# Attention exponentials: values two pairs behind their scores, and a polynomial over 2 x 112 columns in place

## Chip, core and metric

The kernel runs on one core of one Trainium2 chip. The metric is the device time of one launch in microseconds; it is measured in several executions, and one more execution is profiled. The core has five engines with queues of their own: PE (matrix products, into PSUM), ACT (functions such as the exponential), DVE (elementwise work), POOL (elementwise work on SBUF alone, and the issue of some DMAs) and SP (issue of the other DMAs).

## What is computed

The reference mixes attention over 2048 tokens (16 heads of 28 columns) with a mixture of eight experts, by a gate of one number per token:

```python
def _A_ref(x, wqkv, wo):
    B, S, D = x.shape
    H = 16; Dh = D // H
    qkv = (lambda x, *d: x.transpose(*d))((x @ wqkv).reshape(B, S, 3, H, Dh), 2, 0, 3, 1, 4)
    q, k, v = qkv[0], qkv[1], qkv[2]
    scale = Dh ** -0.5
    scores = jnp.einsum("bhqd,bhkd->bhqk", q, k) * scale
    p = _softmax(scores, axis=-1)
    o = jnp.einsum("bhqk,bhkd->bhqd", p, v)
    return (lambda x, *d: x.transpose(*d))(o, 0, 2, 1, 3).reshape(B, S, D) @ wo
...
x = A_x
g = _sigmoid((x * gate_w).sum(-1, keepdims=True))
a = _A_ref(x, A_wqkv, A_wo)
b = _B_ref(x, B_w_gate, B_w1, B_w2)
return g * a + (1 - g) * b
```

The change touches the attention alone: the exponentials of the scores and their product with the values.

## The kernel before

The program first makes q, k and v, then runs the experts (with row maxima of the scores beside them), and then the attention as a stage of its own. The work of the attention is cut into 16 units u: four groups of four heads, and in each four blocks of 512 queries. A unit has eight pairs p of key tiles, a tile being 128 keys; `m` counts the pairs from 0 to 127. The softmax is not normalised in the loop: the row maximum is part of the scores' matmul (a 29th row of K and Q), so the exponential is safe, and a column of ones in V sums it.

For one pair, `scores(m)` writes eight cells of 128 keys x 512 queries (two key tiles, four heads). They go into all eight PSUM banks: for the first key tile the single bank `z[0]` and the three banks of `t[0]`, for the second the three of `t[1]` and the single `z[1]`. Each cell takes three matmul passes (high and low parts of K and Q). ACT then does exp on `z[0]` (L1230), on the three banks of `t[0]` at once (L1231), and on those of `t[1]` (L1239). The cell `z[1]` is copied by DVE into SBUF as `X`, scaled (L1232); of X, ACT does the first 352 columns (L1240), and the last PW = 160 go through a polynomial, `power`: four steps on POOL (L1246 to L1251) that split the exponent off, and four on DVE (L1253, L1254, L1255 and L1257) that evaluate it and write `P[:, 7]`. `P` holds the eight exponentials of a pair and has two buffers.

`values(m)` multiplies P by V into the same single banks `z[0]` (columns 0 to 287 of the queries) and `z[1]` (288 to 511) at L1271, and DVE adds both to the accumulator `osb` of the unit (L1281, or a copy at L1279 for a unit's first pair). So one round on PE is scores of pair m+1, then values of pair m; a single bank goes from scores to ACT's or DVE's read, to values, to DVE's add, and to the next scores.

The order on PE, DVE, ACT and POOL is the order in which the code is written (`manual_schedule`); SP's order is made by the scheduler. Beside the pairs, `beside(m)` places the work of other units: sums of a unit's exponentials go to memory and back to be inverted (`collect_sums`, `slice_sums`, `invert_sums`, `spread_sums`, the last fetching the row `rs`), `divide_half` divides osb by them two units later, `place` stores osb into `OT`, K, V and Q of the next group are loaded (`load_k`, `load_v`, `load_q`), and wo and OT are split into high and low parts. POOL's DMAs wait in the list `due`, from which each `power` takes one behind its third POOL step. At the end stand the 16 projections with wo (L1137).

Of the kernel before, what the change touches and what calls it, by code (L numbers as in the profile page):

```python
# [63 lines left out]
def tile_gated_mha_moe(ctx: ExitStack, tc: tile.TileContext, x, xe_, xT, wv, wqk, wo, w1, w2, out):  # L64
# [1037 lines left out]
    def split_wo_high(b):  # L1102
        nc.vector.tensor_copy(wo_h[:, b], wo_r[b])
# [60 lines left out]
    def divide_half(u, h):  # L1164
        cs = slice(256 * h, 256 * h + 256)
        nc.vector.tensor_tensor(accs[u][:, cs], accs[u][:, cs], rs[u][:, cs], op=ALU.mult)
# [26 lines left out]
    PW = 160  # L1193
# [24 lines left out]
    def scores(m):  # L1218
# [3 lines left out]
        X = sb.tile([128, 512], F32, name="X")  # L1222
        P = sb.tile([128, 8, 512], F32, name="P")
# [6 lines left out]
        nc.scalar.activation(P[:, 0], z[0], AF.Exp, scale=SCALE)  # L1230
        nc.scalar.activation(P[:, 1:4], t[0], AF.Exp, scale=SCALE)  # L1231
        nc.vector.tensor_scalar(X, z[1], LAM * SCALE * math.log2(math.e), -126.0 * LAM, op0=ALU.mult, op1=ALU.max)  # L1232
# [6 lines left out]
        nc.scalar.activation(P[:, 4:7], t[1], AF.Exp, scale=SCALE)  # L1239
        nc.scalar.activation(P[:, 7, 0:512 - w], X[:, 0:512 - w], AF.Exp, scale=math.log(2.0) / LAM)  # L1240
        Pc[m] = [P[:, i] for i in range(8)]

    def power(x, to):
        u, n, g, y = (sb.tile([128, PW], F32, name=f"p{c}", bufs=1 + (c == "u")) for c in "ungy")
# [8 lines left out]
        nc.vector.scalar_tensor_tensor(y, g, EXP2[0], g, op0=ALU.add, op1=ALU.mult)  # L1253
        nc.vector.scalar_tensor_tensor(v, y, EXP2[1], g, op0=ALU.add, op1=ALU.add)  # L1254
        nc.vector.scalar_tensor_tensor(w, y, EXP2[2], v, op0=ALU.add, op1=ALU.mult)  # L1255
        yield
        nc.vector.scalar_tensor_tensor(to, w, EXP2[3], e.bitcast(F32), op0=ALU.add, op1=ALU.mult)  # L1257

    def values(m):
# [13 lines left out]
        if p == 0:  # L1273
            accs[u] = sb.tile([128, 512], F32, name="osb", bufs=4)
        for n, (po, cs) in enumerate(parts):
            if n:
                piece(u, p)
# [4 lines left out]

    def piece(u, p):
        if u > 1 and p in (2, 3):
            divide_half(u - 2, p - 2)

    def beside(m):
# [17 lines left out]
        if p == 0 and 5 <= u < 9:  # L1305
            split_wo_high(u - 5)
# [102 lines left out]
```

## Time and profile before

| | |
|---|---|
| time, median of 3 runs (lowest, highest) | 1333.95 us (1333.61, 1334.13) |
| the profiled execution: its own time | 1334.03 us |
| its span, first to last instruction | 1332.2 us |
| granted clock of TensorE | 1.00 |
| attention stage, first to last L1230 | 833.23 to 1287.97 us |
| mean of L1231 and L1239 (1536 columns) | 1446 and 1460 ns |
| mean of L1230 (512) and L1240 (352) | 600 and 509 ns |
| mean of the four DVE steps of the polynomial | 320, 325, 339, 317 ns |
| mean of the four POOL steps | 353, 329, 545, 375 ns |

The profile gives each instruction's start and duration, and what the idle time of its engine ahead of it waited for ("idle before, releaser"). In a row of groups stand line, engine, operation, output and inputs, shape, count, then busy us, mean ns, and the idle us by releaser. In a row of the timeline stand start and duration in us, then the same names. A duration isn't always what an instruction costs its engine: the next one can start before the former has ended, so distances from start to start are looked at too.

### The profile page before, as it was taken

The numbers are of one execution on the slowest core, as the hardware profiler recorded it, in microseconds if no ns is written. First come the engines' busy times: TensorE is split into PE (matmuls) and PEld (weight loads), VectorE is DVE, ScalarE is ACT, GpSimd is POOL, SyncE is SP. The second block draws the span as 40 slices with busy tenths as digits, with TensorE's granted clock in tenths as the row PEclk, the third lists the DMA queues.
The fourth block names the chain that finished last, engine by engine and source line by source line (L and its number), as shares of the span: only waits on it lengthen the run. The fifth ranks groups of instructions, "written<-read, shape, count | busy, mean of one in ns | idle before, by whom it ended". The sixth has DMA issues, their size and how long they took to land. (4 is left out here: it accounts for less than half of the span.)

```text
span 1332.2 us, 32345 instructions
## 1 busy us (share of the span) xinstructions
PE 1325.2 (99%) x12210; PEld 936.9 (70%) x12210; DVE 1064.0 (80%) x1667; ACT 843.5 (63%) x1271; POOL 856.7 (64%) x1142
## 2 busy tenths in 40 slices
PE   9999999999999999999999999999999999999999
PEld 8888788788887777777777777555555555555558
DVE  5746899888898888989888786777788778777775
ACT  5325454355364344543445434999999999999981
POOL 2143967877787788786887844666666666656641
PEclk9999999999999999999999999999999999999999
DMA  9887657554553475455746423212422432242214
GB/s 349 301 268 267 185 162 187 153 151 109 166 157 86 149 203 149 137 125 155 187 120 184 93 78 68 62 39 64 121 54 70 113 81 49 76 111 54 49 41 137
DMA packets 139520, 176.83 MB, mean 133 GB/s; under 512 B 25576, under 2 KB 107242, under 8 KB 138850
## 3 DMA queue, kind: packets, MB, share of 16 engines
q1 hardware_dynamic: 120626, 145.68, 36.0%
q0 software_dynamic: 18592, 28.84, 10.5%
q8 instruction: 96, 1.57, 0.5%
q14 instruction: 62, 0.51, 0.1%
q10 hardware_dynamic: 144, 0.23, 0.1%
HBM read 124.54 MB, written 53.25 MB: 133 GB/s over the span
## 5 line engine op out<-in xcount | busy, mean ns | idle before, releaser
L149 DVE TENSOR_REDUCE mp<-pm 128x3 f32<-128x1536 f32 (+1 forms) x301 | 508.9, 1733 | 10.9 <-PE pm L128 10.8
L1271 PE MATMUL z<-P,V 128*32 128x288 f32 x4064 | 247.9, 382 | 1.0 <-ACT P L1230 0.2
L1271 PEld LDWEIGHTS z<-P,V 128*32 128x32 f32 x4064 | 110.2, 109 | 132.7 <-ACT P L1230 48.5
L1065 ACT ACTIVATE yo<-acc,cg 128x448 f32<-128x448 f32 x64 | 40.7, 636 | 232.1 <-PE acc L1050 222.7
L833 POOL TENSOR_TENSOR w2l<-w2r,w2h 128x448 fp32r<-128x448 f32 x112 | 130.6, 1167 | 86.1 <-ACT w2h L827 64.9
L762 PE MATMUL s<-Q,Kh 29*128 29x512 f32 x1524 | 185.7, 437 | 0.0
L1239 ACT ACTIVATE P<-s 128x1536 f32<-128x1536 f32 x127 | 185.4, 1460 | 0.0
L1231 ACT ACTIVATE P<-s 128x1536 f32<-128x1536 f32 x127 | 183.6, 1446 | 0.0
L762 PE MATMUL z<-Q,Kh 29*128 29x512 f32 x508 | 182.7, 438 | 0.0
L1050 PE MATMUL acc<-w2h,hh 128*128 128x448 f32 x448 | 167.0, 373 | 0.3 <-PEq L847 0.3
L1050 PE MATMUL acc<-w2h,hl 128*128 128x448 f32 x448 | 166.5, 372 | 0.0
L1050 PE MATMUL acc<-w2l,hh 128*128 128x448 f32 x448 | 166.1, 371 | 0.0
L997 ACT ACTIVATE hf<-acc 128x512 f32<-128x512 f32 (+6 forms) x154 | 74.3, 482 | 136.5 <-PE acc L993 130.6
L142 DVE TENSOR_REDUCE mp<-acc 128x1 f32<-128x512 f32 x130 | 89.5, 688 | 83.9 <-PE pm L128 81.8
L842 POOL TENSOR_TENSOR hl<-hf,hh 128x512 fp32r<-128x512 f32 x112 | 145.9, 1303 | 1.1 <-ACT hh L1000 0.5
L993 PE MATMUL acc<-xeh,w1h 128*128 128x512 f32 (+3 forms) x408 | 136.8, 339 | 0.0
L993 PE MATMUL acc<-xeh,w1l 128*128 128x512 f32 (+3 forms) x408 | 136.1, 338 | 0.0
L1246 POOL TENSOR_SCALAR pu<-X 128x160 f32<-128x160 f32 x126 | 44.4, 353 | 132.7 <-DVE X L1232 131.2
L1281 DVE TENSOR_TENSOR osb<-z,osb 128x288 f32<-128x288 f32 x224 | 95.1, 425 | 41.6 <-PE z L1271 31.9
L1232 DVE TENSOR_SCALAR X<-z 128x512 f32<-128x512 f32 x127 | 87.8, 691 | 44.5 <-PE z L762 30.8
L801 POOL TENSOR_TENSOR w1l<-w1r,w1h 128x1024 fp32r<-128x1024 f32 (+1 forms) x49 | 91.1, 1860 | 43.7 <-ACT w1h L795 24.2
L128 PE MATMUL pm<-khg,qg 28*128 28x512 f32 x894 | 110.5, 449 | 0.9 <-DVE lo L672 0.9
(238 smaller groups left out, 3072.4 us busy)
## 6 DMA issues: line engine op xcount, KB each, us to landing
w2r<-in_w_dram SPq DMA_DIRECT2D x112, 224.0 KB
w1r<-in_w_dram SPq DMA_DIRECT2D x56, 384.0 KB
x_d<-xf SPq DMA_DIRECT2D x115, 64.0 KB
ys_d<-zero_d SPq DMA_DIRECT2D x32, 224.0 KB
qkh_d<-hi SPq DMA_DIRECT2D x28, 256.0 KB
qkl_d<-lo SPq DMA_DIRECT2D x28, 256.0 KB
w1r<-in_w_dram SPq DMA_DIRECT2D x112, 64.0 KB
ys_d<-yo SPq DMA_DIRECT2D x32, 224.0 KB
```

The lines of the kernel that those rows point to most:

```text
L128: nc.tensor.matmul(banks[n], qgs[g, qt // 4][rw, (qt % 4) * 128:(qt % 4 + 1) * 128], kh[g, kc][rw], start=True, stop=True)
L149: nc.vector.tensor_reduce(mp[:, (o + lo) % 256:(o + lo) % 256 + hi - lo], pm[h][:, lo - 3 * h:hi - 3 * h], axis=AX.X, op=ALU.max)
L762: nc.tensor.matmul(banks[j], k[rw, ks], q[rw, c], start=i == 0, stop=i == 2)
L801: nc.gpsimd.tensor_tensor(l[:, :, half], r[:, :, half], h[:, :, half].bitcast(F32), op=ALU.subtract)
L833: nc.gpsimd.tensor_tensor(w2l, w2r, w2h.bitcast(F32), op=ALU.subtract)
L842: nc.gpsimd.tensor_tensor(hl, hf32, hh[:, 0:512].bitcast(F32), op=ALU.subtract)
L993: nc.tensor.matmul(pu[:, 0:HC], a, b[:, cs], start=i == 0, stop=i == len(mms) - 1)
L1050: nc.tensor.matmul(py[:n, 0:D], a[:, cs], b, start=i == 0, stop=i == 3 * NH - 1)
L1231: nc.scalar.activation(P[:, 1:4], t[0], AF.Exp, scale=SCALE)
L1239: nc.scalar.activation(P[:, 4:7], t[1], AF.Exp, scale=SCALE)
L1271: nc.tensor.matmul(po[32 * j:32 * j + 32, cs], v[:, kt % 8, 32 * j:32 * j + 32], P[4 * i + j][:, cs], start=i == 0, stop=i == 1)
L1281: nc.vector.tensor_tensor(accs[u][:, cs], po[:, cs], accs[u][:, cs], op=ALU.add)
```

## The change

The core of the diff (the loop's end, the splitting and the dividing in smaller parts shortened):

```diff
-    PW = 160
+    PW = 112
...
-        X = sb.tile([128, 512], F32, name="X")
-        P = sb.tile([128, 8, 512], F32, name="P")
+        P = sb.tile([128, 8, 512], F32, name="P", bufs=3)
...
-        nc.scalar.activation(P[:, 0], z[0], AF.Exp, scale=SCALE)
-        nc.scalar.activation(P[:, 1:4], t[0], AF.Exp, scale=SCALE)
-        nc.vector.tensor_scalar(X, z[1], LAM * SCALE * math.log2(math.e), -126.0 * LAM, op0=ALU.mult, op1=ALU.max)
+        w = PW if m + 1 < NU * NPR else 0
+        far = t[0].rearrange("p a n -> p (a n)")
+        to = P[:, 1:4].rearrange("p a n -> p (a n)")
+        if m - 2 in powers:
+            next(powers.pop(m - 2), None)
+        if w:
+            nc.vector.tensor_scalar(to[:, 1535 - w:], far[:, 1535 - w:], LAM * SCALE * math.log2(math.e), -126.0 * LAM,
+                                    op0=ALU.mult, op1=ALU.max)
         if m - 1 in powers:
-            next(powers.pop(m - 1), None)
-        w = PW if m + 1 < NU * NPR else 0
+            next(powers[m - 1])
+        nc.vector.tensor_scalar(P[:, 0], z[1], LAM * SCALE * math.log2(math.e), -126.0 * LAM, op0=ALU.mult, op1=ALU.max)
+        if m - 1 in powers:
+            next(powers[m - 1])
         if w:
-            powers[m] = power(X[:, 512 - w:], P[:, 7, 512 - w:])
+            powers[m] = power(P[:, 0:4:3, 512 - w:])
             next(powers[m])
+        nc.scalar.activation(P[:, 7], z[0], AF.Exp, scale=SCALE)
+        nc.scalar.activation(to[:, 0:1536 - w], far[:, 0:1536 - w], AF.Exp, scale=SCALE)
         nc.scalar.activation(P[:, 4:7], t[1], AF.Exp, scale=SCALE)
-        nc.scalar.activation(P[:, 7, 0:512 - w], X[:, 0:512 - w], AF.Exp, scale=math.log(2.0) / LAM)
+        nc.scalar.activation(P[:, 0, 0:512 - w], P[:, 0, 0:512 - w], AF.Exp, scale=math.log(2.0) / LAM)
...
         nc.vector.scalar_tensor_tensor(y, g, EXP2[0], g, op0=ALU.add, op1=ALU.mult)
+        yield
         nc.vector.scalar_tensor_tensor(v, y, EXP2[1], g, op0=ALU.add, op1=ALU.add)
+        yield
         nc.vector.scalar_tensor_tensor(w, y, EXP2[2], v, op0=ALU.add, op1=ALU.mult)
         yield
-        nc.vector.scalar_tensor_tensor(to, w, EXP2[3], e.bitcast(F32), op0=ALU.add, op1=ALU.mult)
+        nc.vector.scalar_tensor_tensor(x, w, EXP2[3], e.bitcast(F32), op0=ALU.add, op1=ALU.mult)
...
-    for m in range(NU * NPR):
-        if m + 1 < NU * NPR:
-            scores(m + 1)
+    for m in range(-1, NU * NPR):
+        if m + 2 < NU * NPR:
+            scores(m + 2)
```

In words. The loop writes the scores of pair m+2 ahead of the values of pair m, and P has three buffers. X is gone: z[1] is copied straight into its place in P, and its exponential is written over it. The polynomial now works on two pieces of 112 columns at once, the last 112 of that cell and the last 112 of the three banks of `t[0]`; DVE copies the latter into P first (113 columns, one of which ACT then overwrites, so that ACT's operation follows DVE's). ACT does 1424 instead of 1536 columns there and 400 instead of 352 of the copied cell. The four DVE steps of a polynomial no longer stand together but between other work. The divide of a unit comes in four parts of 128 columns behind the adds of pairs 2 to 5 instead of two of 256 between the adds of pairs 2 and 3, `place` follows two pairs later, the split of wo's high part comes in halves, osb has three buffers instead of four, and some of the last unit's work stands at other pairs.

On ACT, one pair before, where `z` and `s` are the single and the threefold banks:

```order
L1230 ACTIVATE P<-z_10081 128x512
L1231 ACTIVATE P<-s_10082 128x1536
L1239 ACTIVATE P<-s_10096 128x1536
L1240 ACTIVATE P<-X 128x352
L1230 ACTIVATE P<-z_10148 128x512
```

and one pair now:

```order
L1245 ACTIVATE P<-z_10055 128x512
L1246 ACTIVATE P<-s_10056 128x1424
L1247 ACTIVATE P<-s_10070 128x1536
L1248 ACTIVATE P<-P 128x400
L1245 ACTIVATE P<-z_10123 128x512
```

The order is the same; two of the four shapes differ. On DVE, one round before, with the copy of z[1], the polynomial's last step for the pair ahead, the two adds, and the three first steps of this pair:

```order
L1232 TENSOR_SCALAR X<-z_10027 128x512
L1257 SCALAR_TENSOR_TENSOR P<-pg,pu 128x160
L1281 TENSOR_TENSOR osb<-z_10056,osb 128x288
L1281 TENSOR_TENSOR osb<-z_10057,osb 128x224
L1253 SCALAR_TENSOR_TENSOR py<-pg 128x160
L1254 SCALAR_TENSOR_TENSOR X<-py,pg 128x160
L1255 SCALAR_TENSOR_TENSOR pg<-py,X 128x160
```

and one round now:

```order
L1235 TENSOR_SCALAR P<-s_10124 128x113
L1261 SCALAR_TENSOR_TENSOR py<-pg 128x224
L1239 TENSOR_SCALAR P<-z_10137 128x512
L1263 SCALAR_TENSOR_TENSOR P<-py,pg 128x2x112
L1291 TENSOR_TENSOR osb<-z_10168,osb 128x288
L1265 SCALAR_TENSOR_TENSOR pg<-py,P 128x224
L1291 TENSOR_TENSOR osb<-z_10169,osb 128x224
L1267 SCALAR_TENSOR_TENSOR P<-pg,pu 128x2x112
```

The four steps, all of the pair ahead, now stand one each behind the 113-column operation, the copy, the first add and the second add. On PE at the end of the stage, from the second part of the last scores, before:

```order
L762 MATMUL s_18839<-Q,Kl_16612 128x512 x3
L762 MATMUL z_18838<-Q,Kl_16612 128x512
L1271 MATMUL z_18858<-P,V_16768 32x288 x8
L1271 MATMUL z_18859<-P,V_16768 32x224 x8
L1271 MATMUL z_18880<-P,V_16768 32x288 x4
L1271 MATMUL z_18881<-P,V_16768 32x224 x4
```

and now:

```order
L762 MATMUL s_18834<-Q,Kl_16695 128x512 x3
L762 MATMUL z_18833<-Q,Kl_16695 128x512
L1281 MATMUL z_18855<-P,V_16838 32x288 x8
L1281 MATMUL z_18856<-P,V_16838 32x224 x8
L1281 MATMUL z_18886<-P,V_16838 32x288 x8
L1281 MATMUL z_18887<-P,V_16838 32x224 x8
L1281 MATMUL z_18911<-P,V_16838 32x288 x4
L1281 MATMUL z_18912<-P,V_16838 32x224 x4
```

The values of one more pair (16 matmuls) now stand behind the last scores; the last pair's are cut in four pieces in both.

More of the change, by code (lines that the diff above doesn't have):

```diff
@@ L1100, in fetch_wo, with split_wo_high @@
         nc.sync.dma_start(wo_r[b], wo[:, b])
-    def split_wo_high(b):
-        nc.vector.tensor_copy(wo_h[:, b], wo_r[b])
+    def split_wo_high(b, h):
+        nc.vector.tensor_copy(wo_h[:, b, h], wo_r[b][:, h])
     def split_wo_low(b, h):
@@ L1273, in values @@
         if p == 0:
-            accs[u] = sb.tile([128, 512], F32, name="osb", bufs=4)
+            accs[u] = sb.tile([128, 512], F32, name="osb", bufs=3)
         for n, (po, cs) in enumerate(parts):
-            if n:
-                piece(u, p)
+            if n and m + 1 in powers:
+                next(powers[m + 1])
             if p == 0:
@@ L1281, in values @@
                 nc.vector.tensor_tensor(accs[u][:, cs], po[:, cs], accs[u][:, cs], op=ALU.add)
-    def piece(u, p):
-        if u > 1 and p in (2, 3):
-            divide_half(u - 2, p - 2)
     def beside(m):
@@ L1304, in beside @@
             fetch_wo(u - 4)
-        if p == 0 and 5 <= u < 9:
-            split_wo_high(u - 5)
-        if p in (2, 3) and 5 <= u < 9:
-            split_wo_low(u - 5, HALF[p - 2])
-        if u > 1 and p == 3:
+        if 5 <= u < 9:
+            if p < 2:
+                split_wo_high(u - 5, HALF[p])
+            if p > 5:
+                split_wo_low(u - 5, HALF[p - 6])
+        if u > 1 and 2 <= p < 6:
+            divide_part(u - 2, p - 2)
+        if u > 1 and p == 5:
             place(u - 2)
-        if u and p == (5 if u + 1 < NU else 4):
+        if u and p == (5 if u + 1 < NU else 3):
             invert_sums(u - 1)
@@ L1317, in beside @@
         if u == NU - 1:
-            if p in (0, 4):
-                split_o_high(p // 4, nc.vector)
-            if p in (2, 7):
+            if p in (0, 6):
+                split_o_high(p // 6, nc.vector)
+            if p in (1, 7):
                 split_o_low(p // 7)
-    for m in range(NU * NPR):
-        if m + 1 < NU * NPR:
-            scores(m + 1)
+    for m in range(-1, NU * NPR):
+        if m + 2 < NU * NPR:
+            scores(m + 2)
+        if m < 0:
+            continue
+        if m in powers:
+            next(powers.pop(m), None)
         values(m)
@@ L1332, in tile_gated_mha_moe @@
         beside(m)
-        if m + 1 in powers:
-            next(powers[m + 1])
     collect_sums(NU - 1)
```

10 lines of the change are left out of this document (5 added, 5 removed).

## Prediction

> **What bounds the kernel now.** I read the page first, then the timeline of the attention stage engine by engine, then the groups by shape. The stage runs from the first ACT exponential at 833.23 us to the end of the last values at about 1292.8 us; its 128 pairs of key tiles are the only place the change touches.
>
> ```profile
> PE 1325.2 (99%) x12210; PEld 936.9 (70%) x12210; DVE 1064.0 (80%) x1667; ACT 843.5 (63%) x1271; POOL 856.7 (64%) x1142
> ACT  5325454355364344543445434999999999999981
> 838.00:1284.00 446.00, 445.10 (x6932) 234.56 (x6924) 351.50 (x924) 444.57 (x495) 279.04 (x586) 1.00 0.29 71
> ```
>
> The first two lines are of the page. PE's 99% says little, since a queued matmul counts as busy. ACT is at 63% of the span, but in nine tenths or more of every slice of the attention stage. The third line is the table by stretches: of 446.0 us, ACT was busy 444.6, DVE 351.5 (79%), POOL 279.0 (63%). So ACT looks like the limit. The distance between its starts shows how closely.
>
> ```profile
> 1065.31 1.46 ACT L1239 ACTIVATE P<-s 128x1536 f32<-128x1536 f32 x1
> 1066.64 0.51 ACT L1240 ACTIVATE P<-X 128x352 f32<-128x352 f32 x1
> 1067.13 0.60 ACT L1230 ACTIVATE P<-z 128x512 f32<-128x512 f32 x1
> 1067.62 1.45 ACT L1231 ACTIVATE P<-s 128x1536 f32<-128x1536 f32 x1
> 1068.95 1.46 ACT L1239 ACTIVATE P<-s 128x1536 f32<-128x1536 f32 x1
> 1070.28 0.51 ACT L1240 ACTIVATE P<-X 128x352 f32<-128x352 f32 x1
> 1070.69 0.60 ACT L1230 ACTIVATE P<-z 128x512 f32<-128x512 f32 x1
> ```
>
> ACT instructions overlap by about 0.1 us, so what counts is start to start: 0.49 + 1.33 + 1.33 + 0.41 = 3.56 us a pair from 1067.13 to 1070.69. But ahead of 1067.13 ACT was not back to back: 0.49 us from L1240 to L1230, where 0.41 is enough. It waited for PE there, and the pair still took 3.56. Something other than ACT is just as long. It is a loop through one PSUM bank, z0:
>
> ```profile
> 1001.22 0.50 PE L762 MATMUL z<-Q,Kh 29*128 29x512 f32 x1
> 1002.27 0.60 ACT L1230 ACTIVATE P<-z 128x512 f32<-128x512 f32 x1
> 1002.92 1.93 PE L1271 MATMUL z<-P,V 128*32 128x288 f32 x32
> 1003.13 0.69 DVE L1232 TENSOR_SCALAR X<-z 128x512 f32<-128x512 f32 x1 [0.29 <-PE z L762]
> 1003.74 0.32 DVE L1257 SCALAR_TENSOR_TENSOR P<-pg,pu 128x160 f32<-128x160 f32 x1
> 1004.17 0.46 DVE L1281 TENSOR_TENSOR osb<-z,osb 128x288 f32<-128x288 f32 x1
> 1004.79 0.50 PE L762 MATMUL z<-Q,Kh 29*128 29x512 f32 x1
> 1004.95 0.39 DVE L1281 TENSOR_TENSOR osb<-z,osb 128x224 f32<-128x224 f32 x1 [0.33 <-PE z L1271]
> ```
>
> Scores are written to z0 (1001.22), ACT reads them (1002.27), values go into the same bank (1002.92), DVE adds them to osb (1004.17), and only then may the next scores be written (1004.79). The steps are 1.05 + 0.65 + 1.25 + 0.62 = 3.57 us. So there are two limits, ACT at 3.56 and the z0 loop at 3.57. The mean is above both:
>
> ```profile
> 833.23 0.60 ACT L1230 ACTIVATE P<-z 128x512 f32<-128x512 f32 x1 [0.25 <-PE s L762]
> 1287.97 0.60 ACT L1230 ACTIVATE P<-z 128x512 f32<-128x512 f32 x1
> 1288.62 4.25 PE L1271 MATMUL z<-P,V 128*32 128x288 f32 x64
> 1291.12 0.64 ACT L1240 ACTIVATE P<-X 128x512 f32<-128x512 f32 x1
> 1292.80 0.47 PE L1137 MATMUL s<-wo_h,oh 128*128 128x448 f32 x1
> ```
>
> From the first to the last L1230 there are 126 pairs in 454.74 us: 3.609 us each, 0.04 above the loop. That 0.04 is where the two limits push each other, plus single waits.
>
> **The change, part by part.** *ACT.* From 512 to 1536 columns the distance grows by 0.84 us, 0.82 ns a column. The first three-bank operation loses 112 columns (-92 ns), the copied cell gains 48 (400 instead of 352, +39 ns): 3.56 becomes 3.51 us. *The z0 loop.* None of its four steps changes. Values two pairs behind read another P, but still wait for ACT's read of z0 and for their add. So the pair falls to the loop, **3.57**, and not to ACT's 3.51: 126 x (3.609 - 3.57) = **-4.9 us**, if the single waits go too.
>
> *DVE and POOL*, which now carry 224 columns instead of 160 and one more operation:
>
> ```profile
> L1232 DVE TENSOR_SCALAR X<-z 128x512 f32<-128x512 f32 x127 | 87.8, 691 | 44.5 <-PE z L762 30.8 <-PE s L762 11.9 <-issue 0.3
> L1254 DVE SCALAR_TENSOR_TENSOR X<-py,pg 128x160 f32<-128x160 f32 x126 | 41.0, 325 | 4.3
> L1257 DVE SCALAR_TENSOR_TENSOR P<-pg,pu 128x160 f32<-128x160 f32 x126 | 39.9, 317 | 3.0 <-POOL pu L1251 2.5
> L842 POOL TENSOR_TENSOR hl<-hf,hh 128x512 fp32r<-128x512 f32 x21 | 27.2, 1296 | 0.0
> L1248 POOL TENSOR_TENSOR pg<-pn,X 128x160 f32<-128x160 f32 x126 | 68.6, 545 | 10.5
> L1247 POOL TENSOR_SCALAR pn<-pu 128x160 f32<-128x160 f32 x126 | 41.5, 329 | 10.4
> L1111 POOL DMA_INDIRECT b<-ys_d,slot_i x32 | 46.5, 1453 | 5.8 <-issue 4.5
> ```
>
> On DVE, 325 ns at 160 columns and 691 at 512 give 1.04 ns a column: a polynomial step becomes 392 ns (4 x 67 more), the new 113-column operation costs 276. DVE goes from 351.5 us over 124 pairs (2.83 each) to 3.37 of 3.57: 94% by durations, less by starts, since starts overlap by some 0.08 (L1232 above ends at 1003.82, L1257 starts at 1003.74). It fits if each piece stands where DVE would idle. Three places decide. (a) Ahead of the first add stands the second polynomial step, where L1257 stood: it would run from 1003.74 to 1004.13, and the add begins at 1004.17, when PE has its values. Cover: 0.04 us, and each ns beyond it is paid in every pair. (b) Between the two adds stands the third step, in the 0.32 us idle from 1004.63 to 1004.95: 0.07 too long, or nothing with the overlap. Bank z1, which the second add frees, is wanted some 0.2 us later. (c) The 113-column operation must end before ACT's L1231 position, 0.5 us after L1230. It follows the last step, and the scores it reads are complete about when L1230 starts: 0.28 of 0.5. ACT waits for it, as both write one column; behind ACT's operation stand t[1] and the copied cell, but ACT now has 0.06 spare. I put all three at 0. Divides in four parts of 128 columns and the halves of wo stand behind the second add and use the same slack: 0.
>
> On POOL the two-input step costs (1296 - 545)/352 = 2.13 ns a column, so +136 ns. For the one-input steps no second shape of this type is in the trace; they gain 0 at the least and the two-input 136 at the most. I take half, 68, because one operand is read. That is +0.34 us a pair, 2.25 to 2.59 us of 3.57. POOL is not in the loop: its result is first used a whole round later, behind the next 113-column operation. An indirect DMA of 1.45 us (two in most units of eight pairs) made L1257 late before (the 2.5 us in its row, and its pair's add); that goes, since the last step now has a round more.
>
> *The end.* Before, the last L1230 starts at 1287.97 and the first projection at 1292.80, 4.83 us later: values of pairs 126 and 127 stand behind the last scores. Now those of 125 stand there too. They start 0.65 after L1230, two rounds of values at 1.87 (1002.92 to 1004.79, the bank's turn-round) follow, and the last takes about 1.95: 6.34, **+1.5 us**. ACT's last exponential, at 1291.76, is hidden then. At the start nothing is gained: ACT alone paces the first pairs.
>
> *Single waits that stay or come.*
>
> ```profile
> L186 DVE TENSOR_TENSOR ol<-OT,oh 128x384 fp32r<-128x384 f32 x16 | 8.8, 552 | 2.3 <-ACT oh L1120 2.2
> rs<-inv_d POOLq DMA_DIRECT2D x16, 256.0 KB, 6.5
> 932.98 3.17 SPq L1187 DMA_DIRECT2D OT<-osb  x4
> 945.44 2.52 SPq L733 DMA_DIRECT2D Kl<-qkl_d  x4
> 948.01 1.68 SPq L748 DMA_DIRECT2D Q<-qkh_d  x4
> ```
>
> The split of OT in the last unit (552 ns and a smaller part) exceeds DVE's slack: 0.4. The row rs lands 6.5 us after its issue; issue and first divide both move later by less than 1 us: 0.4 in all. SP's order puts the second half of K behind the stores to OT (3.17 us, waiting for the fourth divide) and the Q loads (three issues of some 1.7). Counted from the start of the round with the group's last scores: the second add ends at 4.1 (1005.34 against 1001.22), the divide at some 4.4; then 3.2 for OT, 3.6 for nine more issues of Q, 2.9 for seven of Kh at Q's 0.42 each, 2.5 for Kl: issued by 16.6, and wanted by the scores five rounds later, at 17.9, with the landing still to come. It lands in time, or with five stores to OT (units 7 and 11) just not: 0 to 3 us over three group changes, and I take 0.4, since the first half has rounds to spare.
>
> **The sum.** -4.9 + 1.5 + 1.2 = -2.2. The profiled execution took 1334.03 us (span 1332.2 and 1.8 around it; 0.08 above the median of 1333.95), so **1331.8 us**.
>
> **Rivals.** *First, DVE and POOL block each other (slower).*
>
> ```profile
> 1007.59 0.33 DVE L1257 SCALAR_TENSOR_TENSOR P<-pg,pu 128x160 f32<-128x160 f32 x1 [0.16 <-POOL pu L1251]
> 1007.63 0.47 POOL L1246 TENSOR_SCALAR pu<-X 128x160 f32<-128x160 f32 x1
> L1246 POOL TENSOR_SCALAR pu<-X x126: 322/335/467, 835.0 to 1286.1; 128x160 f32<-128x160 f32 x126
> ```
>
> [...] By DVE's four steps and POOL's four, the overlapping work per pair is now 1.57 + 1.9 us of 3.57, where it was 1.3 + 1.55. In place (a) the cover is 0.04 us and in (b) 0.2; a step that met one of the other engine's lost 0.13 here. It decides from the point where the wait exceeds this cover. At 0.06 us a pair it costs 7.6: 1331.8 + 7.6 = 1339.4. Against it: POOL's first step starts after the copy, behind the DVE step of place (a), and the other POOL steps find DVE mostly in adds. [...] *Second, the loop also runs at its best (faster).*
>
> ```profile
> 1078.15 0.60 ACT L1230 ACTIVATE P<-z 128x512 f32<-128x512 f32 x1 [0.18 <-ACT P L1240]
> 1081.70 0.60 ACT L1230 ACTIVATE P<-z 128x512 f32<-128x512 f32 x1
> ```
>
> With ACT idle ahead, this pair took 3.55. Then 126 x 0.059 = 7.4 less 1.5 and 0.5 of waits: 1328.6. *Third, the 0.04 was not ACT's* but small waits that only move: nothing is gained but the end costs 1.5 and half a microsecond comes back: about 1335.
>
> **Chances.** Forecast 0.55, first rival 0.18, second 0.15, third 0.12. A measurement of this kernel can tell about 0.2%, 2.7 us, so the same reaches from 1331.3 to 1336.6. The forecast's own range, 1330.4 to 1333.2, crosses the lower bound: 0.22 of it is faster, 0.33 the same. Faster 0.22 + 0.15, same 0.33 + 0.12, slower 0.18. The range takes in the second rival and most of the first: 1328.4 to 1339.0.
>
> **What would show it.** Right: ACT's L1230 position is no longer back to back (gaps of about 0.46 instead of 0.41), pairs at 3.56 to 3.58, the first projection 6.3 us after the last z0 exponential. Wrong: the first add starts more than 1.3 us after the values (place a), scores wait for the second add (b), ACT's first three-bank operation waits for DVE (c), or PE waits for a Kl DMA at units 4, 8 and 12.

## The result and the profile after

| | before | changed |
|---|---|---|
| median of 4 runs, us | 1334.04 | 1352.69 |
| lowest to highest, us | 1333.61 to 1334.73 | 1351.30 to 1355.42 |
| profiled execution: time, span, us | 1334.03, 1332.2 | 1351.30, 1349.4 |
| first to last z0 exponential (126 pairs), us | 454.74 | 469.27 |

The changed kernel is slower: ratio 1.0142, interval 1.0124 to 1.0159. It was forecast at 1331.8 us in a range of 1328.4 to 1339.0. One execution of a later run, e16, took 3179.62 us against 1343.76 to 1349.59 for its three others, and is left out of its figures.

The page of the changed kernel: busy time by engine, ACT's slices, and the chain that ended last by lines:

```profile
PE 1336.0 (99%) x12210; PEld 952.1 (71%) x12210; DVE 1117.7 (83%) x1825; ACT 842.6 (62%) x1271; POOL 905.1 (67%) x1142
ACT  5325354355354443543435445999899989989971
PE z L1281 16%; PE s L762 7%; PE z L762 7%; PE s L1137 1%; PE acc L1050 1%; DMA Kl<-qkl_d 1%; PE z L1137 1%; SPq L1187 1%; SPq L748 1%; SPq L733 0%; SPq L736 0%; SPq L750 0%; ACT P L1247 0%; ACT P L1246 0%; ACT P L1245 0%
```

New in the chain are a transfer, Kl<-qkl_d, and issues of SP (L1187, L748), each rounded to 1% of the span (1% is 13 us). ACT's slices dip to 8 at three places. The table by stretches (PE, PEld, DVE, ACT, POOL):

```profile
838.00:1299.00 461.00, 454.81 (x6936) 248.51 (x6932) 403.40 (x1075) 444.04 (x495) 327.01 (x585) 0.99 0.30 68
```

ACT was busy 444.0 of 461 us, about as many as in the 446 us of before: it waited 15.5 us more. First to last exponential, and the first projection, in the time line:

```profile
834.04 0.60 ACT L1245 ACTIVATE P<-z 128x512 f32<-128x512 f32 x1 [0.25 <-PE s L762]
1303.31 0.60 ACT L1245 ACTIVATE P<-z 128x512 f32<-128x512 f32 x1
1309.71 0.47 PE L1137 MATMUL s<-wo_h,oh 128*128 128x448 f32 x1
```

So 126 pairs took 14.5 us more, and the end 6.40 us instead of 4.83. An ordinary pair is not longer. These are its rows (the z0 loop, and ACT around it):

```profile
1020.76 0.49 PE L762 MATMUL z<-Q,Kh 29*128 29x512 f32 x1
1021.48 0.54 ACT L1248 ACTIVATE P<-P 128x400 f32<-128x400 f32 x1
1021.91 0.60 ACT L1245 ACTIVATE P<-z 128x512 f32<-128x512 f32 x1
1022.39 1.37 ACT L1246 ACTIVATE P<-s 128x1424 f32<-128x1424 f32 x1
1022.56 1.93 PE L1281 MATMUL z<-P,V 128*32 128x288 f32 x32
1023.62 1.48 ACT L1247 ACTIVATE P<-s 128x1536 f32<-128x1536 f32 x1
1023.81 0.46 DVE L1291 TENSOR_TENSOR osb<-z,osb 128x288 f32<-128x288 f32 x1
1024.42 0.50 PE L762 MATMUL z<-Q,Kh 29*128 29x512 f32 x1
1024.95 0.57 ACT L1248 ACTIVATE P<-P 128x400 f32<-128x400 f32 x1
1025.49 0.60 ACT L1245 ACTIVATE P<-z 128x512 f32<-128x512 f32 x1
```

Start to start, 1021.91 to 1025.49, it is 3.58 us; the median of all 126 distances is 3.579 (before: 3.584). From values to the add 1.25 us, to the next scores 1.86: as before. The 14.5 us stand at the three changes of group, that is where the scores pass from one group of four heads to the next and need its K. The exponentials at the first and third of them, and what PE, DVE and ACT waited for at the first:

```profile
960.07 0.60 ACT L1245 ACTIVATE P<-z 128x512 f32<-128x512 f32 x1
...
961.59 0.50 PE L762 MATMUL s<-Q,Kl 28*128 28x512 f32 x1 [1.03 <-DMA Kl<-qkl_d]
962.34 0.50 PE L762 MATMUL s<-Q,Kl 28*128 28x512 f32 x1 [0.26 <-DMA Kl<-qkl_d]
...
962.95 0.28 DVE L1235 TENSOR_SCALAR P<-s 128x113 f32<-128x113 f32 x1 [3.16 <-PE s L762]
963.26 1.36 ACT L1246 ACTIVATE P<-s 128x1424 f32<-128x1424 f32 x1 [2.59 <-DVE P L1235]
...
967.99 0.60 ACT L1245 ACTIVATE P<-z 128x512 f32<-128x512 f32 x1 [1.61 <-PE s L762]
...
1201.08 0.60 ACT L1245 ACTIVATE P<-z 128x512 f32<-128x512 f32 x1 [1.48 <-PE z L762]
1209.33 0.60 ACT L1245 ACTIVATE P<-z 128x512 f32<-128x512 f32 x1 [2.82 <-PE z L762]
```

The pair took 7.92 us instead of 3.58, those at the next two changes 8.11 and 8.25; at the second and third the pair ahead took 4.08 and 5.09 as well. Together that is 15.5 us above 3.58. PE waits for the second half of K. The chain has 5.59 us of transfer behind SP's last issue, and SP's queue, in the time line from 940 to 960 us, shows how late that issue was:

```profile
956.71 5.59 DMA Kl<-qkl_d
```

The queue itself:

```profile
942.21 0.31 SPq L733 DMA_DIRECT2D Kh<-qkh_d  x1
942.62 1.20 SPq L748 DMA_DIRECT2D Q<-qkh_d  x3
945.11 3.18 SPq L1187 DMA_DIRECT2D OT<-osb  x4
...
948.95 2.98 SPq L748 DMA_DIRECT2D Q<-qkl_d  x4
951.97 1.14 SPq L750 DMA_DIRECT2D Q<-m_d  x4
...
955.47 1.64 SPq L733 DMA_DIRECT2D Kl<-qkl_d  x4
958.61 0.40 SPq L720 DMA_DIRECT2D V<-v_d  x1
```

One piece of K leaves at 942.21, then the four stores to OT (which wait for the last divide until 945.11) and the Q loads go first, and the last Kl piece is issued by 957.11. It was at hand at 962.3, which is called its landing below. In the kernel before the same half left between 941.5 and 948.0, ahead of Q.

### The profile page after: what moved, and what is told of

It is laid out like the page before. It is cut to its first block, busy times and chain, and to the rows that moved or that the text cites. A ratio compares the mean times of both kernels' runs of the same rounds, so it can differ in the third digit from the quotient of the medians.

```text
span 1349.4 us, 32385 instructions
## 1 busy us (share of the span) xinstructions
PE 1336.0 (99%) x12210; PEld 952.1 (71%) x12210; DVE 1117.7 (83%) x1825; ACT 842.6 (62%) x1271; POOL 905.1 (67%) x1142
## 3 DMA queue, kind: packets, MB, share of 16 engines
q8 instruction: 96, 1.57, 0.5%
## 5 line engine op out<-in xcount | busy, mean ns | idle before, releaser
L1281 PEld LDWEIGHTS z<-P,V 128*32 128x32 f32 x4064 | 118.9, 110 | 132.7 <-ACT P L1245 53.3
L1247 ACT ACTIVATE P<-s 128x1536 f32<-128x1536 f32 x127 | 185.1, 1457 | 0.0
L762 PE MATMUL s<-Q,Kh 29*128 29x512 f32 x1524 | 182.6, 428 | 2.0 <-DMA Kh<-qkh_d 0.8
L762 PE MATMUL z<-Q,Kh 29*128 29x512 f32 x508 | 178.0, 428 | 0.0
L1246 ACT ACTIVATE P<-s 128x1424 f32<-128x1424 f32 (+1 forms) x127 | 172.1, 1355 | 8.6 <-DVE P L1235 8.4
L1254 POOL TENSOR_SCALAR pu<-P 128x224 f32<-128x224 f32 x126 | 55.4, 440 | 99.6 <-DVE P L1239 97.3
L762 PE MATMUL s<-Q,Kl 28*128 28x512 f32 x762 | 108.7, 394 | 3.4 <-DMA Kl<-qkl_d 3.2
```

The costliest lines, as they stand in the source:

```text
L762: nc.tensor.matmul(banks[j], k[rw, ks], q[rw, c], start=i == 0, stop=i == 2)
L1246: nc.scalar.activation(to[:, 0:1536 - w], far[:, 0:1536 - w], AF.Exp, scale=SCALE)
L1281: nc.tensor.matmul(po[32 * j:32 * j + 32, cs], v[:, kt % 8, 32 * j:32 * j + 32], P[4 * i + j][:, cs], start=i == 0, stop=i == 1)
```

## The experiments

Each ratio below is to the kernel before, run on the same chip beside it. e1 to e4, e5 to e8, e9 to e12, e13 to e16, and e17 with e18 each shared a chip, on which the kernel before took 1334.7, 1338.1, 1334.3, 1334.3 and 1340.3 us. Where a pair is named by p, the distances between the z0 exponentials are meant, counted from 0 in each eight. The rival theories: the late K half (A), a loss spread over all pairs (B), and a new wait that takes K's place (C).

**e1: the K half ahead in the queue.**

```diff
-            if p == 6:
+            if p == 5:
                 held[g + 1][0][1] = load_k(g + 1, 1)
```

> The changed kernel with the load of the next group's second K half given out one pair earlier, so that it stands ahead of the OT stores and the Q loads in SP's queue; nothing else moves. Theory A (the second K half is late at three group changes): PE's waits for Kl vanish at the three group changes, the three periods of 7.9 to 8.3 us and the 4.1 and 5.1 us ones fall to 3.6 to 3.7, and the time falls by the 15.5 us that they hold above 3.58: 1352.7 to about 1337 (1335 to 1339). The median pair stays 3.58. Theory B (the loss is spread over all pairs: DVE and POOL in each other's way, or the longer polynomial): the time stays above 1348. Theory C (the K half moves, and the Q loads or the OT stores become late in its place): the wait for Kl is gone, another wait of 2 to 4 us stands at the group changes, 1341 to 1348.

Measured: 1336.45 us, ratio 1.0014 (1.0004 to 1.0023). SP's queue now:

```profile
942.56 0.31 SPq L733 DMA_DIRECT2D Kh<-qkh_d  x1
...
945.23 1.60 SPq L733 DMA_DIRECT2D Kl<-qkl_d  x4
946.93 3.18 SPq L1187 DMA_DIRECT2D OT<-osb  x4
950.16 2.71 SPq L748 DMA_DIRECT2D Q<-qkh_d  x4
```

No wait for K is left, the median pair is 3.580, and 16.2 us are gone by one number in the code (15.3 against e2, which ran on the same chip with the changed kernel's queue). A holds; B and C fall. What remains is 1.8 us more than before.

**e2: V's second half later.**

```diff
-        if g and qc == 0 and p == 0:
+        if g and qc == 0 and p == 2:
             held[g][1][1] = load_v(g, 1)
```

> The changed kernel with the load of V's second half, which stands right behind the late K half in SP's queue, given out two pairs later; the K half stays where it was. If the K half is late because V's 1 MB travels with it (its last piece landed some 5.2 to 5.6 us after its issue, a time in which V's packets were moving too), its landing falls to 1.5 to 2 us, the wait at each of the three group changes falls from about 4.4 to about 1 us and the time to about 1342 (1339 to 1345). If the place in the queue alone makes it late, the landing and the time stay as they were: 1350 to 1355.

Measured: 1351.71 us, 1.0123 (1.0106 to 1.0140). It tested nothing: SP's queue kept its order, and V left at 957.71, right behind Kl (958.61 in the changed kernel). Giving the load out two pairs later in the program did not move it; nothing that waits came to stand ahead of it.

**e3: divides and OT stores early.**

```diff
-        if u > 1 and 2 <= p < 6:
-            divide_part(u - 2, p - 2)
-        if u > 1 and p == 5:
+        if u > 1 and p in (2, 3):
+            divide_part(u - 2, 2 * p - 4)
+            divide_part(u - 2, 2 * p - 3)
+        if u > 1 and p == 3:
             place(u - 2)
```

> The changed kernel with the divides of a unit's sums in pairs p = 2 and 3 (256 columns each) and its OT stores at p = 3, where the kernel before had them; the K half stays behind the Q loads, but the OT stores no longer stand ahead of it. The four stores took 3.2 us of SP's queue, so the K half is issued some 3.2 us sooner. If a landing takes 5.5 us as before, the waits fall from about 4.4 to about 1.2 us at each of three changes and the smaller ones behind them vanish: 1352.7 - 11 = about 1342 (1339 to 1345). If the sooner issue also takes the landing out of V's way, all 15.5 us go: 1337. If the stores' place does not matter: 1350 to 1355.

Measured: 1339.33 us, 1.0034 (1.0023 to 1.0045). The last Kl piece was issued by 954.43, 11.3 us after the first piece instead of 14.9, and no wait for K is left at any of the three changes. So the place of the OT stores and of the divides that must come first, which the change moved from p = 3 to p = 5, is worth 13.4 of the 18.7 us (12.4 against e2 on the same chip). With two divides in a row the pairs at p = 4 take 3.73 (median) instead of 3.58, and just behind the second change a divide waited 1.9 us for rs, in a pair of 5.39; that is most of what e3 lacks against e1.

**e4: the kernel before, K behind Q.**

```diff
-            if p == 6:
+            if p == 7:
                 held[g + 1][0][1] = load_k(g + 1, 1)
...
-        if u > 1 and p == 3:
+        if u > 1 and p == 7:
             place(u - 2)
```

> The kernel before with the second K half given out one pair later, so that it stands behind the Q loads in SP's queue, and with the OT stores at p = 7; nothing of the polynomial or of the distance of values to scores is touched. Twelve Q transfers take 5.2 us of SP's queue, so the last K piece is issued about 12.5 us after the start of the pair with the group's last scores, and wanted at about 18. With a landing of up to 5.5 us it comes just in time: 1334 to 1336, no wait for Kl above 0.5 us. If the time goes up by more than 3 us with waits for Kl, the Q loads alone make the K half late.

Measured: 1343.60 us, 1.0074 (1.0057 to 1.0091): 9 us slower and no wait for K, which neither side had expected. The three pairs at the changes took 4.85, 7.95 and 7.91 us for another transfer; at the second change:

```profile
1068.07 0.77 POOL L1162 DMA_DIRECT2D rs<-inv_d  x1
1077.43 0.43 DVE L1166 TENSOR_TENSOR osb<-osb,rs 128x256 f32<-128x256 f32 x1 [2.98 <-DMA rs<-inv_d]
1078.21 0.18 PEld L762 LDWEIGHTS z<-Q,Kh 29*128 29x128 f32 x1 [2.60 <-DVE osb L1281]
```

The spread of the sums (rs, 256 KB) landed 9.4 us after its issue (the median of this run is 5.6), with K and V beside it, and the divide, which the kernel before has between its two adds, held the second add and with it PE. That K's and V's packets made it late is argued from the times; no run took them away.

**e5 to e8, on another chip.** e5 gives out POOL's gathers at p = 1 and 3; e6 is e1 with the cut of the values at 256, e7 the kernel before with that cut, e8 is e1 with 80 columns a cell by polynomial.

```diff
-        if u + 1 < NU and p in (4, 6):
-            due.append(lambda t=u + 1, c=p // 2 - 2: fetch_routed(t, c))
+        if u + 1 < NU and p in (1, 3):
+            due.append(lambda t=u + 1, c=p // 2: fetch_routed(t, c))
...
-    CA = 288
+    CA = 256
...
-    PW = 112
+    PW = 80
```

> The changed kernel with POOL's two gathers of the routed rows of each unit given out at p = 1 and 3 instead of 4 and 6; SP's queue stays as in the changed kernel, the late K half included. Between 955.0 and 956.5 us of the changed kernel's profile the packets of the second gather moved and almost none of the K half. Theory A1 (the landing of 5 us is partly that gather's share of the transfer engines): the last Kl piece lands 1.5 to 2 us sooner, the periods of 7.9 to 8.3 us fall to 6 to 6.5, those of 4.1 and 5.1 to 3.6, the time to about 1345 (1343 to 1348). Theory A2 (only SP's order counts, the landing is what these transfers take anyway): periods and time stay, 1350 to 1355.

> The kernel of e1_k_first with the query columns of the values cut at 256 instead of 288, so that z0's bank gets fewer value columns and its add is shorter. If the pair is bound by the z0 loop (1.05 + 0.65 + 1.25 + 0.62 = 3.57 us, of which the 1.25 shrinks by about 0.12), the median pair falls from 3.58 to ACT's 3.51 to 3.53 and the time by 6 to 8 us, to about 1329 (1327 to 1332). If DVE's own load binds it (its work is the same in sum), the median stays at 3.58 and the time at 1335 to 1338.

> The kernel before with the same cut at 256. There ACT needs 3.56 us a pair start to start, 0.02 less than the median pair: by the loop theory the pair can fall only to ACT's 3.56, and the time stays at 1332 to 1335. If ACT's 3.56 is no limit in its own right, the time falls by as much as in the changed kernel, 6 to 8 us, to 1326 to 1329. Slower than 1337 would mean that the larger z1 part costs something of its own.

> The kernel of e1_k_first with 80 columns of each cell by polynomial instead of 112: ACT does as many columns as in the kernel before (1456 + 432 = 1536 + 352), and DVE's and POOL's polynomial work shrinks from 224 to 160 columns, again as before. If the pair is bound by the z0 loop, ACT's relief was worth nothing and the median pair stays at 3.57 to 3.58; if besides DVE's longer steps make the pairs of 3.64 to 3.96 us (those with a divide, a reciprocal or a half of wo), these fall to 3.58 and the time by 2 to 4 us, to 1332 to 1335. If ACT's relief was worth its 0.05 us, the median pair rises to 3.60 or more and the time to 1339 or more.

Measured: e5 1362.03 us, 1.0180 (1.0152 to 1.0209); e6 1349.18, 1.0079 (1.0062 to 1.0096); e7 1344.42, 1.0043 (1.0029 to 1.0057); e8 1340.79, 1.0018 (1.0008 to 1.0027). No time came out as expected, and one reason lies in none of the edits. A pair of e6 with a gather:

```profile
987.24 1.67 POOL L1111 DMA_INDIRECT b<-ys_d,slot_i  x1 [0.15 <-issue]
987.53 0.60 ACT L1245 ACTIVATE P<-z 128x512 f32<-128x512 f32 x1
...
988.62 0.69 DVE L1239 TENSOR_SCALAR P<-z 128x512 f32<-128x512 f32 x1 [0.46 <-PE z L762]
```

DVE's copy of z1 starts 1.09 us after the exponential; in pairs without a gather it is 0.72. In the 32 pairs with a gather the median is 1.14 in e6, 1.15 in e5, 0.98 in e8; in e1 it is 0.72 with a gather and 0.73 without. The pair is then 3.9 us (median of e5 and e6; 3.68 in e8). In the rows above DVE and PE's scores into z1 were done 0.46 us before the copy began, so it waited for something else. e5's three long pairs were 5.35, 8.00 and 11.66 us, no shorter in sum than the changed kernel's, although no gather moved beside K: against A1. e8 stays level with e1 (1.0018 against 1.0014), its median pair 3.580, and ACT is now back to back:

```profile
1020.41 0.57 ACT L1248 ACTIVATE P<-P 128x432 f32<-128x432 f32 x1
1020.88 0.60 ACT L1245 ACTIVATE P<-z 128x512 f32<-128x512 f32 x1
1024.45 0.60 ACT L1245 ACTIVATE P<-z 128x512 f32<-128x512 f32 x1
```

From L1248 to L1245 it is 0.47 us for 432 columns, where the changed kernel had 0.54 for 400 (1024.95 to 1025.49): there ACT waited a little, here it does not, and the pair is the same. ACT's limit in e8 and the z0 loop's in e1 lie within 0.01 us of each other. In e7 the pairs at even p took 3.66 to 3.77 (medians); of the 32 pairs with a gather 30 stand at p = 0 and 6, and what makes those at 2 and 4 long is open.

**e9 to e12: the same again beside each other.** e9 is the changed kernel, e10 is e1, e11 is e6; e12 is e1 with plain loads for the gathers:

```diff
-        nc.gpsimd.indirect_dma_start(out=b1s[t], out_offset=None, in_=ys_d,
-                                     in_offset=bass.IndirectOffsetOnAxis(ap=slot_i[:, c, t:t + 1], axis=0),
-                                     **({"compute_op": ALU.add} if c else {}))
+        nc.gpsimd.dma_start(b1s[t], ys_d[t * 128:t * 128 + 128], **({"accum_op": ALU.add} if c else {}))
```

> The changed kernel itself, beside the next three on one chip. In the runs e5 to e8 the kernel before took 1338.0 us, 3.4 more than beside e1 to e4, and in their 32 pairs with one of POOL's gathers DVE's copy of z1 began 0.25 to 0.4 us late, which it did in none of the runs beside 1334.7. If that belongs to the chip, all four kernels of this call agree: with a kernel before near 1334.7 no copy is late and the changed kernel takes 1351 to 1355; with one near 1338 the copies are late and it takes 1358 to 1365. If it belongs to the edits of e5 to e8, the changed kernel shows no late copy and 1351 to 1355 either way.

> The kernel of e1_k_first, beside the others of this call. Theory A (the late K half holds all of the loss): 15 to 16 us below e9_change_again on the same chip, and within 0.3% of the kernel before. If late copies in the pairs with a gather cost the changed kernel more than the kernel before on some chips: 8 to 12 us above the kernel before there.

> The kernel of e6_k_first_ca256, beside the kernel with the cut at 288 (e10). In e6 the first add ended 0.14 us earlier, and PE began the next scores no earlier: it was still at the values of z1. If PE's order alone binds the pair (values of both parts, 1.87 us, between the exponential of z0 and the next scores, whatever the cut), it takes the same as e10 within 2 us and the median pair is 3.58. If the larger z1 part costs time of its own (e6 was 11 us above the kernel before, e1 only 2), it is 5 us or more above e10.

> The kernel of e1_k_first with POOL's gathers of routed rows replaced by plain loads of as many bytes from fixed rows; the output then holds the wrong expert rows, and POOL has 1.0 us less to do in each of 32 pairs (a gather takes 1.3 to 1.4 us, a plain issue 0.6 to 0.8). If the gathers' late copies are in play on this chip, the copy starts at 0.72 us after the exponential in all pairs and the time is 8 to 10 us below e10; if not, the time is that of e10 within 2 us.

Measured: e9 1353.24 us, 1.0135 (1.0110 to 1.0159); e10 1336.30, 1.0014 (1.0005 to 1.0024); e11 1336.93, 1.0016 (1.0006 to 1.0026); e12 1335.15, 1.0007 (0.9998 to 1.0017). The kernel before took 1334.3 and no copy is late in any (0.72 us in e9, e10 and e11): e6's 11 us belonged to where it ran, not to the cut. A is confirmed a second time: 16.9 us between e9 and e10. With the copies on time the cut is worth nothing, and the rows say why; first e10 (288), then e11 (256):

```profile
1021.23 1.94 PE L1281 MATMUL z<-P,V 128*32 128x288 f32 x32
1022.47 0.46 DVE L1291 TENSOR_TENSOR osb<-z,osb 128x288 f32<-128x288 f32 x1 [0.18 <-PE z L1281]
1023.09 0.49 PE L762 MATMUL z<-Q,Kh 29*128 29x512 f32 x1
```

```profile
1022.02 1.93 PE L1281 MATMUL z<-P,V 128*32 128x256 f32 x32
1023.16 0.42 DVE L1291 TENSOR_TENSOR osb<-z,osb 128x256 f32<-128x256 f32 x1
1023.88 0.49 PE L762 MATMUL z<-Q,Kh 29*128 29x512 f32 x1
```

The add begins 1.24 us after the values in the one, 1.14 in the other; the next scores begin 1.86 us after them in both. In e10 the profile names the add as what released the scores, and they follow its end by 0.157 to 0.161 us in nine pairs of ten, as in the changed kernel. In e11 the add ended 0.30 us before them (1023.58) and they came no sooner. PE goes through the values of both parts before it comes to the scores, and that way is just as long: behind the add stands a second limit of the same length.

**e13 to e18: why the landing was so long.** All but e16 are the changed kernel with K still late. e13 leaves out V's second half, e14 the lists of indices (the diff of e12: plain loads of the same bytes), e15 both; e17 moves the spread of the sums, e18 is e17 and e13 together.

```diff
-            held[g][1][1] = load_v(g, 1)
+            held[g][1][1] = held[g - 1][1][1]
...
+        change = qc == 3 and g + 1 < NG
+        if change and p == 3:
+            due.append(lambda: spread_sums(u - 1, u - 2))
-        if u and u + 1 < NU and p == 7:
+        if u and u + 1 < NU and p == 7 and not change:
             due.append(lambda: spread_sums(u - 1))
```

> The changed kernel without the load of V's second half at the three group changes (the first group's half is used again, so the output holds wrong values for half of the keys of groups 1 to 3). The K half stays behind the OT stores and the Q loads; nothing of 512 KB follows it any more. If V's packets make the landing long, the last Kl piece lands 1.5 to 2.5 us after its issue instead of 5, the three long periods fall to 5 us or less, and the time from about 1353 to 1343 (1340 to 1346). If the gather ahead of it or the engines' rate makes it, 1349 to 1355.

> The changed kernel with POOL's gathers replaced by plain loads of as many bytes from fixed rows (the output holds wrong expert rows); the K half stays late and V behind it. In the changed kernel the gather's packets left almost no room for the K half for 1.5 us. A plain load has the same bytes, so: if the bytes make the pause, the time stays at 1349 to 1355; if it is the gather's slow small transfers, the landing shortens by 1 to 1.5 us at each change and the time falls by 3 to 6 us, to 1347 to 1350.

> Both edits of e13 and e14 together. If the two add up, 13 to 16 us below the changed kernel, 1337 to 1341, and hardly a wait for Kl left. If the place in the queue and the engines' rate make the landing whatever stands around it, 1349 to 1355. In between, the difference to e13 and e14 gives each its share.

> The changed kernel with POOL's spread of the sums moved away from the K half at the three group changes: there it is given out at p = 3 and reads the sums of the unit before (they are at hand then; the output has wrong scales in three units). SP's queue stays, the K half is as late in its issue. If the spread's packets hold up the last K pieces, these land within 2 us of the last issue, about 1 us after PE wants them; the periods of 7 to 11 us fall to 4.5 to 5.5, and the time from about 1353 to 1342 (1339 to 1345). If the engines' rate alone makes the landing, 1349 to 1355.

> The edits of e17 and of e13 together: no spread and no V beside the K half at the three group changes (wrong scales, and wrong values for half of the keys). If the spread is the cause, the time is that of e17 or at most 2 us less. If V has a share once the spread is gone, it is 3 us or more below e17. If neither matters, both are at 1349 to 1355.

| run | us (ratio, interval) | three long pairs, us | landing after the last issue, us |
|---|---|---|---|
| changed kernel | 1352.69 (1.0142, 1.0124 to 1.0159) | 7.92, 8.11, 8.25 | 5.2, 5.5, 5.6 |
| e9, the same | 1353.24 (1.0135, 1.0110 to 1.0159) | 9.77, 11.52, 6.77 | 5.7, 7.4, 5.7 |
| e5, gathers moved ahead of K | 1362.03 (1.0180, 1.0152 to 1.0209) | 5.35, 8.00, 11.66 | 4.5, 5.5, 6.6 |
| e13, no V | 1350.45 (1.0118, 1.0084 to 1.0152) | 9.28, 5.05, 9.74 | 5.3, 4.4, 5.4 |
| e14, no index lists | 1358.26 (1.0178, 1.0161 to 1.0195) | 10.90, 11.30, 11.52 | 6.9, 6.8, 6.8 |
| e15, neither | 1356.47 (1.0172, 1.0151 to 1.0193) | 8.27, 10.59, 9.28 | 4.9, 5.5, 4.8 |
| e17, spread away | 1352.37 (1.0097, 1.0075 to 1.0120) | 5.10, 5.05, 5.02 | 4.7, 4.5, 5.2 |
| e18, spread and V away | 1349.84 (1.0087, 1.0058 to 1.0115) | 4.91, 4.20, 4.52 | 4.5, 3.7, 2.1 |

The last column is the last wait for K that ended, less the end of SP's last Kl issue. e17 and e18 ran beside a kernel before of 1340.3 us, and their copies are late as in e5 and e6 (1.16 us in the pairs with a gather), so their times are not to be set beside the others; the pairs are. (e5 had late copies too, and its pairs stayed long.) The long pairs of e17 are as expected, between 4.5 and 5.5, and the loss above 3.58 at the changes is 5.3 us instead of 15.5 and 19.2 (changed kernel and e9). The landing itself shrank less, and not to the 2 us that were expected. At the first two changes K is 1.2 and 1.5 us less late than in the changed kernel; 0.7 and 0.6 of it come from PE wanting it later there (from the last issue's end to the exponential 3.67 and 3.55 us, in the changed kernel 2.96 and 2.99), and only the rest from the landing. Compare the pair of the changed kernel, where K came 2.3 us after the exponential at 960.07 and the pair lost 4.3, with this one (e17's exponentials at the first change, and PE's last wait in the chain):

```profile
964.62 0.60 ACT L1245 ACTIVATE P<-z 128x512 f32<-128x512 f32 x1
969.72 0.60 ACT L1245 ACTIVATE P<-z 128x512 f32<-128x512 f32 x1
```

```profile
960.56 5.08 DMA Kl<-qkl_d
...
965.68 0.50 PE s L762 x3
```

K came 1.06 us after the exponential and the pair lost 1.5; at e9's second change it came 4.9 after and the pair lost 7.9. Counted in this way a microsecond of lateness costs 1.4 to 2.7 us in these runs, and 2.9 and 4.2 at the third changes of e9 and of the changed kernel, where the pair ahead was long already. One reading, argued from the rows: behind the scores that lack K, PE's queue holds values that need no K, DVE's 113-column operation (3.16 us of wait) and ACT's first operation (2.59) stand still too, and all start again one after another.

Packets a microsecond at the first change, by size: K (2 KB), gather (1792 B), spread (4 KB), V (512 B).

```
changed kernel   K  gather  spread   V        e17    K  gather  spread   V
955              1      37       0    0       959   51      20       0    0
956             42      82       0    0       960    2      83       0    0
957            107       3       0    0       961  106      25       0    0
958            104       0       4    0       962  100       0       0   15
959             74       0       8   18       963   68       0       0  150
960              9       0      12  153       964    6       0       0  321
961              0       0      15  244       965    0       0       0  486
```

While a gather moves, K's packets all but stop for about a microsecond, in both. Then K moves at some 105 packets, 210 KB, a microsecond. The seven pieces that remain after the first are 784 KB, so at that rate they alone take 3.7 us. In e5 no gather moved beside K at any change. At the second, the last gather packet had started by 1068.7 and the seven pieces were issued from 1075.6 to 1079.4:

```
e5               K  gather  spread   V
1077            62       0       0    0
1078            69       0       0    0
1079           128       0       0    0
1080            72       0      12    5
1081             8       0      12  146
1082             3       0      14  308
1083             4       0      15  295
1084             1       0      11   75
```

There is no pause, and the landing is no shorter. So the pause is not what makes the landing long. What is long is the tail: in every run of the table 95% of the seven pieces' 392 packets have ended by 1.3 to 3.4 us after the last issue, and a few follow one by one. Beside the spread the last of them ended 3.5 to 6.6 us after the issue, without it (e17 and e18) 2.3 to 4.3. Against the changed kernel e17 lands 0.4 to 1.0 us sooner, e18 0.7 to 3.5. V alone (e13) and the index lists (e14, e15) are not seen to make the long pairs. That e14 and e15 are 3 to 6 us slower than the changed kernel was not expected. In e14 the spread began 0.2 to 0.5 us ahead of the end of K's last issue, in the changed kernel 0.7 to 1.3 behind it, so that more of it lay beside K; that this is why is argued. So the landing is argued to be K's rate (the 210 KB a microsecond above) with the spread's tail on top, and V's where no spread is. No run leaves out gather, spread and V together, so the shares stay open.

**e16: the reciprocal in a pair of its own.**

```diff
-        if u and p == (5 if u + 1 < NU else 3):
+        if u and p == (6 if u + 1 < NU else 3):
             invert_sums(u - 1)
...
-        if u + 1 < NU and p in (4, 6):
-            due.append(lambda t=u + 1, c=p // 2 - 2: fetch_routed(t, c))
+        if u + 1 < NU and p in (4, 5):
+            due.append(lambda t=u + 1, c=p - 4: fetch_routed(t, c))
```

> The kernel of e1_k_first with the reciprocal of the sums one pair later (p = 6, where no divide stands), and the second gather one pair earlier so that POOL's transfers keep their order. If the reciprocal and a divide in one pair make the following pairs 3.66 us (11 of 15 units), those fall to 3.58 and the time by 11 x 0.08 = 0.9 us, to 1335.4; a difference of that size is at the edge of what the rounds can tell, so the pairs decide: median of p = 7 at 3.58. If they stay at 3.66, something else makes them.

Measured: 1348.98 us, 1.0092 (1.0067 to 1.0118), where e10 took 1336.30; the kernel before took 1334.3 beside both. The pairs at p = 7 stayed at 3.66, so the reciprocal does not make them; and the edit brought a wait of its own, since the second gather adds onto the rows of the first and now stood one pair behind it:

```profile
POOL b L1111 <- DMA b<-ys_d,slot_i: 13.1, 12, 3.6
```

## Why the prediction was wrong, step by step

- **ACT falls to 3.51 us a pair: right within 0.04.** 0.48 + 1.23 + 1.33 from the rows above, and 0.43 where L1248 and L1245 stand back to back (1021.48 to 1021.91): 3.47.
- **The pair falls to the z0 loop, 3.57: right in length, wrong as a gain.** The median pair is 3.579, but it was 3.584 before. The -4.9 us was the mean's distance to the loop, and it hung on "if the single waits go too". They did not: in e10, without the K waits, 126 pairs took 454.24 us instead of 454.74, 0.5 less. This step was over-sized by 4.4 us. Before, 32 pairs above 3.61 hold 4.0 us over 3.58. Fifteen of them, at p = 0 and with a gather, take 3.68, as the last polynomial step waits for POOL there (the 2.5 us of L1257's row). In e10 the pairs at p = 0 take 3.58, as the prediction has it, but 28 pairs at other places hold 3.6 us, nine of them at p = 7 with 3.66. e11 adds to the reading: PE's own order is as long as the link through the add.
- **Places (a), (b) and (c) at nothing: right** on the chips where the kernel before took 1334. The add begins 1.25 us after the values, ACT's first operation hardly waits for DVE outside the changes (three times, 1.1 us in all, in e1). In means of e1, the 113-column operation took 0.27 us (forecast 0.276), the four polynomial steps 0.41, 0.38, 0.40 and 0.43 (0.392), POOL's two-input step 0.72 (0.681), and its three others 0.44, 0.39 and 0.47, which is 0.06 to 0.10 more than before (0.068).
- **The end, +1.5 us: right,** 1.57.
- **The second K half, 0.4 us of "0 to 3": the step that failed.** Its issue was right (by 16.6 us after the start of the pair with the group's last scores; its last piece was issued by 16.4 at the first change, from a start at 940.7, and by 16.7 and 16.1 at the others), and so was the time at which it is wanted (17.9; 18.2). But the landing was written down as "still to come" and then counted as if it were short. It took 5.2 to 5.6 us, and the three changes cost 15.5 us. The prediction named this sign of being wrong itself, waits for Kl at units 4, 8 and 12, and there they stand. The rows for a bound stood in the prediction: rs, 256 KB, lands 6.5 us after its issue. 16.6 + 6.5 - 17.9 is 5.2 us late at each of three changes, 16 us in all, and the range ought to have reached there.
- **rs, 0.4: right in the changed kernel** (two waits, 0.7 us), although its landing rose from 6.5 to 8.5 us in the median. The split of OT, also put at 0.4, cost about 0.2: the last unit's pairs hold 0.92 us above 3.58, before 0.76.

In the profiled execution 15.5 (K) less 1.0 (all other pairs) and 1.6 (the end) and 0.8 (a stage that began later, though nothing ahead of it was changed; in e10 it began at 833.43) make 16.9 of the 17.2 us of span.

Rival one, DVE and POOL in each other's way, is not seen in the length of a pair (median 3.579 us) where the kernel before takes 1334: mean durations are as forecast within 0.04 us, and so are the adds. Single POOL steps do vary, L1259 from 0.37 to 0.63 us in the changed kernel. Where it takes 1338 and 1340, DVE is held up, but only in pairs with a gather. Rival three, waits that only move and "about 1335", is what the kernel is once K comes in time: 1336.3 to 1336.5. The change then moves nothing out of the path: ACT's relief is worth nothing, as e8 shows by giving it back, and the two pairs of distance cost 1.6 us at the end. No version tried beats the kernel before.

## What to carry to other kernels

When a step moves, go through each queue that its transfers stand in and write down issue, landing and want as three numbers; take the landing from the longest row of a transfer of that size under load, not from the shortest. Here a transfer that became late cost more than its lateness (1.4 to 4.2 us for each microsecond); that this is because other work stood behind what waited for it is argued from the rows above. And before a gain is read out of a mean, look at the median: here the typical pair already ran at its limit (3.584 us at the median, the mean 3.609), and the mean's excess belonged to single pairs; where the change made some of them short, others became long.

## What was not expected of the hardware

While a gather's 128 rows of 1792 B move, another queue's 2 KB packets become few: 1 and 42 in the first and second microsecond above, 107 in the third. A plain load of as many bytes does the same (e14, second change: 0 and 14, then 118). They do not always stop: at the third change of the changed kernel 48 move in the same microsecond as 76 of the gather. The packets are not counted by engine here, and no run shows what makes the pause.

The spread moved in 64 packets of 4 KB, at most 15 a microsecond at 0.26 us each (mean) in the first change of the changed kernel: 3.9 us of packet time in a microsecond, so by estimate some four moved at a time. At the three changes its packets took 5.8 to 6.3 us from first to last, at the other units but the last 3.1 to 4.5, so it was slowed as well.

On the chips where the kernel before took 1338 and 1340, DVE's copy of z1 starts 0.16 to 0.43 us late in the 32 pairs with a gather (medians of e5 to e8, e17 and e18), and those pairs take 3.7 to 3.95 us instead of 3.58; where it took 1334, it does not. e6 and e11 are the same kernel, with ratios of 1.0079 and 1.0016: the first alone would have been read as the effect of its edit. What the copy waits for is open.
